# On-chip tiles of an attention and feed-forward kernel begin at multiples of 128 bytes

## The chip, the cores and the metric

The kernel runs on one core of one Trainium2 chip, as one program. The metric is the device time of one execution in microseconds (us). Before the change three runs took 1151.57, 1152.28 and 1153.96 us, a median of 1152.28 us.

## The reference

Attention over 4 batches, 12 heads, 448 positions and a head size of 64, with a root-mean-square norm of queries and keys, and then two feed-forward layers over the 1792 tokens of width 768, each with 2048 hidden columns:

```python
q_n, k_n = rmsnorm(q, g_q), rmsnorm(k, g_k)
attn = softmax(q_n @ k_n.T / sqrt(64))          # per batch and head
x = (attn @ v) as [1792, 768]
for w_in, w_out, beta in ((moe), 1.0), ((moe2), 1.702):
    h = x @ w_in
    x = (h * sigmoid(beta * h)) @ w_out
```

The weights come as 8-byte floats and are narrowed to 4 bytes on the chip; all else is 4-byte floats.

## The kernel before

**Stages.** Attention works through 24 pairs of heads (`NP`), and the feed-forward part through eight turns (u, p, g): layer u, half p of the tokens, half g of the hidden columns. While attention and the first turns run, the weights are loaded, narrowed (`block_narrow`), combined (`block_sum`) and stored to DRAM; each turn fetches them back in chunks of 128x768 through a ring of three (`fetch`, tiles f, wh, wl).

**Matmuls of the feed-forward part.** A 4-byte product is made of three matmuls of the type fp32r: every operand is split into a high part and a low part (wh, wl of the weights; th, tl of the first layer's input; bh, bl of the hidden values), and low x high, high x low and high x high are added up in PSUM. All of them are 128x128 weights (stationary) by 128x448 values (moving). Phase one of a turn (`one`, L857) forms seven sums of blocks in the order 1, 6, 2, 7, 5, 4, 3, with 28 tasks of nine matmuls, 252 in a turn; its moving tiles are th1 and tl1 for the first four tasks, th6 and tl6 for the next four, then th2, th7, th5, th4, th3 with their low parts. Phase two has 252 matmuls as well (`two`, L1009), in six turns, and 288 in the other two, the turns with u = 0 and g = 0 (`add_plain`, L952); there bh0 to bh3 and bl0 to bl3 are the moving tiles. That is 2016 + 1512 + 576 = 4104 fp32r matmuls. Of those of L857, 8 turns x 8 tasks x 9 = 576 have one of th1, tl1, th6 and tl6 as the moving tile.

**Attention's matmuls** (L626 scores, L730 values, the transposes at L691 to L705) are plain 4-byte matmuls, not fp32r.

**Order.** The kernel records tasks with estimated lengths, orders them in `emit`, and issues each engine's instructions in that order; the order is fixed when the program is built and nothing of it depends on addresses.

**Where tiles lie.** Pools grow from the left end of a partition (const, xp, wt, ring, rv, ap, then mw) or from its right end (sp, then tp and mg), and each tile begins at the next multiple of 32 bytes. The small tiles gcol, epsc (const), y (ap) and rr (ap), and ms and w (sp) have lengths that are no multiples of 128 bytes, and so set the begin of everything behind them. The usable length ends 32 bytes short of a multiple of 128. In the built program the begins are, as remainders of a division by 128 bytes:

| tiles | before | with the change |
|---|---|---|
| acc, t2, th1, tl1, th6, tl6 (left) | 64 | 0 |
| f, wh, wl, r of the weights; rows r0 to r11 of phase one and two | 64 | 0 |
| th2 to th5, th7 and their low parts (right) | 96 | 0 |
| bh0 to bh3, bl0 to bl3, g (right) | 96 | 0 |
| qk, sq, t, v, kn of attention (right) | 96 | 0 |
| e, ec, at, nb, rb of attention (left) | 32, 0 or 96 by tile | 0 |

Among attention's tiles at0 to at5 begin at 32 and at6 at 0, and rb0 (even pairs) at 0 and rb1 (odd pairs) at 96. In the feed-forward part th1 and th6 lie at 49,600 to 71,104 bytes of a partition and the weights at 74,176 to 98,752, while the b tiles begin at 137,952 or later and th2 and those behind it at 175,584 or later. Slices of a tile that matmuls read (448 moving columns, 128 columns of weights) are 1792 and 512 bytes, both multiples of 128.

Of the kernel before, what the change touches and what calls it, by code (L numbers as in the profile page):

```python
# [10 lines left out]
F32 = mybir.dt.float32  # L11
# [17 lines left out]
def kernel(  # L29
# [20 lines left out]
    NG = 2 * NK + 1  # L50
# [20 lines left out]
    def left(name):  # L71
        return ctx.enter_context(tc.tile_pool(name=name, bufs=1, reuse_waits="tile"))

    const = left("const")
# [5 lines left out]
    dp = ctx.enter_context(tc.tile_pool(name="dp", bufs=1, space=bass.MemoryType.DRAM))  # L80
    attn, early = ExitStack(), ExitStack()
    ap = attn.enter_context(tc.tile_pool(name="ap", bufs=1, reuse_waits="tile"))
    sp = early.enter_context(tc.tile_pool(name="sp", bufs=1, side="right", reuse_waits="tile"))

    ident = const.tile([128, 128], F32, name="ident")
    gcol = const.tile([128, 3], F32, name="gcol")
    epsc = const.tile([128, 1], F32, name="epsc")
    acc = xp.tile([128, NP2, KT, 2, 2 * HS], F32, name="acc")
    layers = ((moe_w_in, moe_w_out), (moe2_w_in, moe2_w_out))

    def engine(c):
        return {"p": nc.gpsimd, "v": nc.vector}[c]
# [4 lines left out]
    def bank(z):  # L97
        return ps.tile([128, 512], F32, tag=f"b{z}", name=f"b{z}")
# [3 lines left out]
    def task(eng, took, fn, reads=(), writes=(), lag=0.1, shared=False):  # L102
        x = len(todo)
        after = set()
        for r in reads:
            after |= {writer[r]} if r in writer else set()
        for r in writes:
            after |= {writer[r]} if r in writer else set()
            after |= readers.get(r, set())
        for r in reads:  # L110
            readers.setdefault(r, set()).add(x)
        for r in writes:
            writer[r], readers[r] = x, set()
        todo.append((eng, took, fn, sorted(after - {x}), lag, shared))
        return x
# [76 lines left out]
    held = {}  # L192
# [207 lines left out]
    def group(m):  # L400
        c, i = divmod(m, 2)
        return NK if c == NK else c + (NK + 1) * i

    def tile_of(key, pool, shape, dtype, tag):
        held[key] = pool.tile(shape, dtype, tag=tag, name=tag)
        return held[key]
# [30 lines left out]
    def norm(p, sides=(0, 1)):  # L437
        s = p % 2
        eng = "v" if p == 0 else "p"
        of = slice(sides[0], sides[-1] + 1)  # L440
        took = {"v": 0.27, "p": 0.56}[eng] * len(sides)

        def tiles():
            if 1 in sides:
                tile_of(("sq", p), sp, [128, 2, NG, D], F32, f"sq{s}")
                tile_of(("ms", p), sp, [128, 2, NG], F32, f"ms{s}")
                tile_of(("w", p), sp, [128, 2, NG], F32, f"w{s}")
                tile_of(("y", p), ap, [128, 2, NG], F32, f"y{p % 4}")

        def square(i):  # L450
            def fn():
                if i == sides[-1]:
                    tiles()
                t = held["qk", p].rearrange("p (i g d) -> p i g d", i=2, d=D)[:, i]
                engine(eng).tensor_tensor(held["sq", p][:, i], t, t, op=ALU.mult)
            return fn

        def fold():
            sq = held["sq", p][:, of]
            engine(eng).tensor_tensor(  # L460
                sq[:, :, :, :D // 2], sq[:, :, :, :D // 2], sq[:, :, :, D // 2:], op=ALU.add
            )

        def total():
            nc.vector.tensor_reduce(
                held["ms", p][:, of], held["sq", p][:, of, :, :D // 2], axis=AX.X, op=ALU.add
            )

        def root():
            w, y = (held[z, p][:, of] for z in "wy")  # L470
            nc.scalar.activation(
                out=w, in_=held["ms", p][:, of], func=ACTF.Ln, scale=1.0 / D, bias=epsc
            )
            nc.scalar.activation(out=y, in_=w, func=ACTF.Exp, scale=-0.5)

        def polish():
            ms, y, w = (held[z, p][:, of] for z in ("ms", "y", "w"))
            e = engine(eng)
            e.tensor_scalar(ms, ms, -0.5 / D, -0.5 * EPS, op0=ALU.mult, op1=ALU.add)
            e.tensor_tensor(w, y, y, op=ALU.mult)  # L480
            e.tensor_tensor(w, w, ms, op=ALU.mult)
            e.tensor_tensor(w, w, y, op=ALU.mult)
            e.tensor_scalar(y, y, 1.5, 0.0, op0=ALU.mult, op1=ALU.add)
            y, w = (held[z, p] for z in "yw")
            for i in reversed(sides):
                o = ry[(p + 1) % 2][:, 8:8 + NG] if i else y[:, 0]
                e.tensor_tensor(o, y[:, i], w[:, i], op=ALU.add)

        ms, y, sq = ([(*z, i) for i in sides] for z in (("ms", s), ("y", p % 4), ("sq", s)))
        for i in reversed(sides):  # L490
            task(eng, 0.535 if p == 0 else 1.11, square(i), reads=[("qk", s, i)], writes=[("sq", s, i)],
                 shared=True)
        task(eng, 2 * took, fold, writes=sq, shared=True)
        task("v", 0.27 * len(sides), total, reads=sq, writes=ms)
        task("a", 0.5, root, reads=ms, writes=y)
        task(eng, 0.75, polish, writes=ms + y + [("ryk", (p + 1) % 2)] * (1 in sides))
# [112 lines left out]
    def scores(p, c):  # L609
        nonlocal turns_s  # L610
        s = p % 2
        heads = range(1 if c == NK else 2)
        zs = [(turns_s + i) % 5 for i in heads]
        turns_s += len(zs)

        def mm():
            if c == 0:
                tile_of(("rr", p), ap, [128, 3, 8], F32, f"rr{p % 3}")
            pss = [bank(z)[:, :S] for z in zs]
            for i, t in enumerate(pss):  # L620
                held["s", p, 2 * c + i] = t
            t = held["t", p]
            cols = slice(128 * c, 128 * c + 128)
            for i, x in enumerate(pss):
                a = slice(0, 128) if c == NK else slice(64 * i, 64 * i + 64)
                nc.tensor.matmul(x, t[a, cols], t[a, NQ:], start=True, stop=True)  # L626

        task("pe", 0.76 if c == NK else 0.82, mm, reads=["ap"] + [("t", p % 4, y) for y in range(3)],
             writes=[("bank", z) for z in zs])
        for i, z in zip(heads, zs):  # L630
            m = 2 * c + i

            def top(m=m):
                nc.vector.tensor_reduce(  # L634
                    held["rr", p][:, 0, group(m):group(m) + 1], held["s", p, m], axis=AX.X,
                    op=ALU.max, negate=True,
                )

            def bias(m=m):
                g = slice(group(m), group(m) + 1)  # L640
                nc.gpsimd.tensor_tensor(  # L641
                    held["rr", p][:, 1, g], held["rr", p][:, 0, g], held["y", p][:, 0, g],
                    op=ALU.mult,
                )

            def exp(m=m, i=i):
                if c == NK:
                    o = tile_of(("ec", p), ap, [128, S], F32, f"ec{s}")
                else:
                    if i == 0:  # L650
                        tile_of(("e", p, c), ap, [128, 2, S], F32, f"e{s}{c}")
                    o = held["e", p, c][:, i]
                g = slice(group(m), group(m) + 1)
                nc.scalar.activation(  # L654
                    out=o, in_=held["s", p, m], func=ACTF.Exp, scale=held["y", p][:, 0, g],
                    bias=held["rr", p][:, 1, g], accum_out=held["rr", p][:, 2, g],
                )

            b, r = ("bank", z), ("rr", p % 3, m)
            task("v", 0.53, top, reads=[b, "ap"], writes=[r])  # L660
            task("p", 0.08, bias, reads=[("y", p % 4, 0)], writes=[r], lag=0.15)
            task("a", 0.72, exp, reads=[b, r, ("y", p % 4, 0), "ap"] + [("e", s, c, 0)] * i,
                 writes=[("e", s, c, z) for z in range(i, 2)] + [("sum", p % 3, m)])
# [502 lines left out]
```

## Time and profile before

| | |
|---|---|
| three runs | 1151.57, 1152.28, 1153.96 us (median 1152.28) |
| the profiled execution | 1150.59 us, of which its span is 1148.8 us |
| granted TensorE clock, mean | 0.992 of full speed |
| PE busy | 1110.5 us, 97% of the span |
| VectorE (DVE) busy | 929.3 us, 81% |
| ScalarE (ACT), GpSimd (POOL) busy | 724.5 us (63%), 380.8 us (33%) |
| feed-forward part | from 293.9 us of the span to its end |

The profile counts an instruction as busy from start to end, and matmuls of one engine overlap: a 128x448 matmul has a length of some 0.37 us, while the next begins some 0.2 us after it began. What a matmul costs where they follow each other without a gap is therefore read from starts, as the distance from one to the next, or from a piece of the chain of waits, whose length is divided by the matmuls in it. Rows of the chain give the start in the span, the length in us, and what ran. PEld is the load of the weights of the next matmul; L12 is line 12 of the kernel before.

### The profile page before, as it was taken

The page shows a single profiled execution, that of the slowest core. Times are in us where ns is not written, and L with a number is a line of the kernel's source. Part 1 is how long each engine was busy: PE and PEld are TensorE (multiplying, and loading weights), DVE is VectorE, ACT ScalarE, POOL GpSimd, SP SyncE. Part 2 cuts the span into 40 slices and gives each one's busy share as a digit, 9 for nine tenths or more (in the row PEclk, how much of TensorE's full clock was granted, in tenths as well). Part 3 has the DMA queues.
Part 4 walks back from the last instruction along what each step waited for, and adds up shares of the span by engine and source line. Part 5 has one row for each costly group of instructions (what it writes and reads, how often), then busy time and mean ns, then how long its engine had stood idle before and what let it go on. Part 6 is the DMA issues. An engine that isn't in the chain of part 4 may idle for free.

```text
span 1148.8 us, 17403 instructions
## 1 busy us (share of the span) xinstructions
PE 1110.5 (97%) x5601; PEld 914.6 (80%) x5601; DVE 929.3 (81%) x1448; ACT 724.5 (63%) x1371; POOL 380.8 (33%) x617
## 2 busy tenths in 40 slices
PE   4899899999999999999999999999999999999998
PEld 2454455555799999899999999999999999999997
DVE  5778888778796679997675999979989885885698
ACT  4677888888676676754766785366566544554452
POOL 5766666533221223314221100614212040420152
PEclk8899999999999999999999999999999999999999
DMA  7677887885747775567777656584583363333333
GB/s 238 187 258 222 272 266 227 253 263 189 236 137 245 240 235 155 162 205 238 250 244 239 211 178 200 155 266 145 185 254 104 122 195 105 102 107 113 99 108 124
DMA packets 178509, 222.09 MB, mean 193 GB/s; under 512 B 12329, under 2 KB 172274, under 8 KB 178418
## 3 DMA queue, kind: packets, MB, share of 16 engines
q1 hardware_dynamic: 178418, 220.98, 61.2%
q8 instruction: 44, 0.72, 0.3%
q14 instruction: 47, 0.39, 0.1%
HBM read 173.57 MB, written 47.36 MB: 192 GB/s over the span
## 4 chain that ended last, share of the span: by engine, by line
PE 77%; DVE 8%; DMA 6%; ACT 3%; issue 2%; POOL 2%; SPq 1%; DVEq 0%; ACTq 0%; POOLq 0%
PE b L857 35%; PE b L1009 22%; PE b L952 10%; PE b L626 3%; PE b L730 3%; DMA rb<-i 2%; PE b L705 2%; ACT e L654 1%; DVE bl L922 1%; DVE rr L634 1%; DVE wl L379 1%; DMA w<-r 1%; DMA i<-rt 1%; PE b L703 1%; DVE at L710 1%
## 5 line engine op out<-in xcount | busy, mean ns | idle before, releaser
L375 ACT CAST wh<-f 128x768 fp32r<-128x768 f32 x212 | 177.0, 835 | 155.2 <-PE b L857 96.6
L379 DVE TENSOR_TENSOR wl<-f,wh 128x768 fp32r<-128x768 f32 x212 | 227.7, 1074 | 55.1 <-ACT wh L375 51.6
L918 ACT CAST bh<-g 128x448 fp32r<-128x448 f32 x232 | 131.0, 566 | 111.0 <-PE b L1009 75.0
L922 DVE TENSOR_TENSOR bl<-g,bh 128x448 fp32r<-128x448 f32 x232 | 166.0, 727 | 41.2 <-ACT bh L918 39.3
L1009 PE MATMUL b<-bl,wh 128*128 128x448 f32 x504 | 186.2, 369 | 0.8 <-DVE bl L922 0.8
L1009 PE MATMUL b<-bh,wl 128*128 128x448 f32 x504 | 186.0, 369 | 0.3 <-DVE r L1035 0.2
L1009 PE MATMUL b<-bh,wh 128*128 128x448 f32 x504 | 185.6, 368 | 0.0
L238 POOL TENSOR_TENSOR r<-r 128x192 f32<-128x192 f32 x100 | 94.0, 945 | 258.7 <-DVE r L222 181.5
L857 PE MATMUL b<-th,wl 128*128 128x448 f32 x672 | 174.9, 369 | 0.0
L857 PE MATMUL b<-tl,wh 128*128 128x448 f32 x672 | 174.7, 369 | 0.0
L857 PE MATMUL b<-th,wh 128*128 128x448 f32 x672 | 174.6, 368 | 0.0
L857 PEld LDWEIGHTS b<-th,wl 128*128 128x128 f32 x672 | 126.5, 188 | 12.2 <-issue 0.7
L857 PEld LDWEIGHTS b<-th,wh 128*128 128x128 f32 x672 | 126.6, 188 | 11.6
L857 PEld LDWEIGHTS b<-tl,wh 128*128 128x128 f32 x672 | 126.6, 188 | 11.5
L905 POOL TENSOR_TENSOR g<-g,g 128x448 f32<-128x448 f32 x39 | 63.0, 1622 | 187.2 <-DVE g L905 100.9
L654 ACT ACTIVATE e<-b,rr,y 128x448 f32<-128x448 f32 x144 | 103.3, 721 | 18.8 <-POOL rr L641 18.5
L634 DVE TENSOR_REDUCE rr<-b 128x1 f32<-128x448 f32 x168 | 97.0, 615 | 19.7 <-PE b L626 19.4
L1009 PEld LDWEIGHTS b<-bl,wh 128*128 128x128 f32 x504 | 95.0, 188 | 11.0 <-DVE bl L922 2.3
L626 PE MATMUL b<-t 64*128 64x448 f32 (+1 forms) x336 | 99.1, 591 | 4.4 <-ACT e L654 3.6
L1009 PEld LDWEIGHTS b<-bh,wl 128*128 128x128 f32 x504 | 95.0, 188 | 9.9 <-DVE r L1035 1.0
L1009 PEld LDWEIGHTS b<-bh,wh 128*128 128x128 f32 x504 | 95.0, 188 | 8.7
L881 ACT ACTIVATE g<-g 128x448 f32<-128x448 f32 x96 | 54.8, 576 | 43.5 <-DVE g L877 43.3
(101 smaller groups left out, 1769.5 us busy)
## 6 DMA issues: line engine op xcount, KB each, us to landing
f<-w SPq DMA_DIRECT2D x212, 384.0 KB
r<-in_moe_w_in SPq DMA_DIRECT2D x64, 384.0 KB
w<-r SPq DMA_DIRECT2D x128, 192.0 KB
r<-in_moe_w_out SPq DMA_DIRECT2D x64, 384.0 KB
w<-r SPq DMA_DIRECT2D x56, 288.0 KB
t<-in_qkt SPq DMA_DIRECT2D x24, 480.0 KB
qk<-in_qk SPq DMA_DIRECT2D x48, 224.0 KB
v<-in_v SPq DMA_DIRECT2D x24, 256.0 KB
```

Source lines behind the costliest of these rows:

```text
L238: engine(e).tensor_tensor(x[:, o], x[:, a], x[:, b], op=op)
L375: nc.scalar.copy(held[w][0], held[f])
L379: nc.vector.tensor_tensor(l, held[f], f32(h), op=ALU.subtract)
L626: nc.tensor.matmul(x, t[a, cols], t[a, NQ:], start=True, stop=True)
L634: nc.vector.tensor_reduce(held["rr", p][:, 0, group(m):group(m) + 1], held["s", p, m], axis=AX.X, op=ALU.max, negate=True,)
L654: nc.scalar.activation(out=o, in_=held["s", p, m], func=ACTF.Exp, scale=held["y", p][:, 0, g], bias=held["rr", p][:, 1, g], accum_out=held ...
L857: nc.tensor.matmul(held[pb], x[:, c0:c0 + 128], y[:, k], start=bool(start and c == 0), stop=(c == 3 * KH - 1), skip_group_check=True,)
L905: engine(e).tensor_tensor(held[o], held[x], held[y], op=op)
L918: nc.scalar.copy(held[r][0], held[src])
L922: nc.vector.tensor_tensor(l, held[src], h.bitcast(F32), op=ALU.subtract)
L952: nc.tensor.matmul(held["plain", z], x[:, ms], y, start=(q == 0 and t == 0 and c == 0), stop=(q == GROUP - 1 and t == 1 and c == 2), skip_ ...
L1009: nc.tensor.matmul(held["p", 5 if i == 3 else i, m], x[:, c0:c0 + 128], y, start=(i != 3 and q2 == 0 and c == 0), stop=(q2 == GROUP - 1 an ...
```

## The change

Five edits, and nothing else: a pad of 24 words at the right end of the partition (`side`), so that the right-hand tiles begin 96 bytes lower; gcol and epsc leave the pool const and share a padded tile of 32 words in ap (`small`), so that acc and what follows begin 64 bytes lower; the tiles ms, w and y become 4x8 words, of which 2x7 are used as before; and rr becomes 4x8 words in place of 3x8.

```diff
     ap = attn.enter_context(tc.tile_pool(name="ap", bufs=1, reuse_waits="tile"))
+
+    ident = const.tile([128, 128], F32, name="ident")
+    side = ctx.enter_context(tc.tile_pool(name="side", bufs=1, side="right", reuse_waits="tile"))
+    side.tile([128, 24], F32, name="side")
     sp = early.enter_context(tc.tile_pool(name="sp", bufs=1, side="right", reuse_waits="tile"))
-
-    ident = const.tile([128, 128], F32, name="ident")
-    gcol = const.tile([128, 3], F32, name="gcol")
-    epsc = const.tile([128, 1], F32, name="epsc")
+    small = ap.tile([128, 32], F32, name="small")
+    gcol, epsc = small[:, 0:3], small[:, 3:4]
     acc = xp.tile([128, NP2, KT, 2, 2 * HS], F32, name="acc")
...
                 tile_of(("sq", p), sp, [128, 2, NG, D], F32, f"sq{s}")
-                tile_of(("ms", p), sp, [128, 2, NG], F32, f"ms{s}")
-                tile_of(("w", p), sp, [128, 2, NG], F32, f"w{s}")
-                tile_of(("y", p), ap, [128, 2, NG], F32, f"y{p % 4}")
+                for z, pool, tag in (("ms", sp, s), ("w", sp, s), ("y", ap, p % 4)):
+                    t = tile_of((z, p), pool, [128, 4, 8], F32, f"{z}{tag}")
+                    held[z, p] = t[:, :2, :NG]
...
-                tile_of(("rr", p), ap, [128, 3, 8], F32, f"rr{p % 3}")
+                tile_of(("rr", p), ap, [128, 4, 8], F32, f"rr{p % 3}")
```

No engine gets another order, another count of instructions or another wait: row by row the programs differ only in the names gcol and epsc (now small) and in the shape of the few norm instructions that read or write ms, w and y, which is 128x2x7 in place of 128x14 (L465, L471, L474 and L479 to L483, once for each of 23 pairs).

## Rows read from the trace of the kernel before

**Rows 1.** The page: span and busy time of each engine.

```profile
span 1148.8 us, 17403 instructions
...
PE 1110.5 (97%) x5601; PEld 914.6 (80%) x5601; DVE 929.3 (81%) x1448; ACT 724.5 (63%) x1371; POOL 380.8 (33%) x617
```

**Rows 2.** The page: the chain that ended last, by engine and by line.

```profile
PE 77%; DVE 8%; DMA 6%; ACT 3%; issue 2%; POOL 2%; SPq 1%; DVEq 0%; ACTq 0%; POOLq 0%
PE b L857 35%; PE b L1009 22%; PE b L952 10%; PE b L626 3%; PE b L730 3%; DMA rb<-i 2%; PE b L705 2%; ACT e L654 1%; DVE bl L922 1%; DVE rr L634 1%; DVE wl L379 1%; DMA w<-r 1%; DMA i<-rt 1%; PE b L703 1%; DVE at L710 1%
```

**Rows 3.** The chain in order of time: start us, length us, engine, line, count.

```profile
349.42 59.52 PE b L952 x288
408.94 51.79 PE b L857 x252
460.73 8.80 PE b L1009 x43
...
484.45 27.88 PE b L1009 x138
...
623.65 36.93 PE b L857 x180
...
699.12 19.69 PE b L1009 x95
...
779.78 52.08 PE b L1009 x252
```

**Rows 4.** Timeline of PE, th6 then (from 423.37) th2: start us, length us.

```profile
421.54 0.77 PE L857 MATMUL b<-th,wl 128*128 128x448 f32 x3
422.15 0.77 PE L857 MATMUL b<-tl,wh 128*128 128x448 f32 x3
422.76 0.77 PE L857 MATMUL b<-th,wh 128*128 128x448 f32 x3
423.37 0.78 PE L857 MATMUL b<-th,wl 128*128 128x448 f32 x3
423.99 0.78 PE L857 MATMUL b<-tl,wh 128*128 128x448 f32 x3
```

**Rows 5.** Timeline of PE, th1 in the first turn.

```profile
295.22 0.78 PE L857 MATMUL b<-th,wh 128*128 128x448 f32 x3
295.84 0.78 PE L857 MATMUL b<-th,wl 128*128 128x448 f32 x3
```

**Rows 6.** Timeline of PE, L1009 around a wait in the second turn.

```profile
482.48 0.37 PE L1009 MATMUL b<-bh,wh 128*128 128x448 f32 x1
482.69 0.37 PE L1009 MATMUL b<-bl,wh 128*128 128x448 f32 x1
...
485.17 0.36 PE L1009 MATMUL b<-bh,wl 128*128 128x448 f32 x1
485.37 0.36 PE L1009 MATMUL b<-bh,wh 128*128 128x448 f32 x1
```

**Rows 7.** Timeline of PEld, the loads of weights in that stretch.

```profile
485.17 0.19 PEld L1009 LDWEIGHTS b<-bh,wh 128*128 128x128 f32 x1
```

**Rows 8.** Windows of turns two and four: us, PE, PEld, DVE, ACT, POOL busy.

```profile
409.00:512.20 103.20, 103.04 (x505) 94.68 (x504) 95.81 (x141) 69.94 (x117) 31.28 (x26) 1.00 0.60 191
...
623.50:727.90 104.40, 104.25 (x506) 94.83 (x505) 96.44 (x161) 70.83 (x117) 8.88 (x7) 1.00 0.62 196
```

**Rows 9.** Costliest groups, by shape: the low parts of the weights.

```profile
L379 DVE TENSOR_TENSOR wl<-f,wh 128x768 fp32r<-128x768 f32 x212 | 227.7, 1074 | 55.1 <-ACT wh L375 51.6 <-DMA f<-w 0.3
```

**Rows 10.** One line each, L730 and L738: duration ns min/median/max.

```profile
L730 PE MATMUL b<-at,v x384: 538/540/591, 41.7 to 304.2; 128*64 128x448 f32 x192
...
L738 DVE TENSOR_TENSOR acc<-b,rb x24: 611/624/626, 45.2 to 304.8; 128x448 f32<-128x448 f32 x24
```

**Rows 11.** Groups by shape: small POOL instructions of the norm.

```profile
L481 POOL TENSOR_TENSOR w<-w,ms 128x14 f32<-128x14 f32 x23 | 5.6, 244 | 1.8
...
L487 POOL TENSOR_TENSOR y<-y,w 128x7 f32<-128x7 f32 x23 | 5.0, 219 | 0.0
```

## The prediction, made before the changed kernel ran

> **What bounds the kernel now.** I read the page first: PE is busy for 1110.5 of 1148.8 us, VectorE (DVE) for 929.3 [rows 1]. The chain that ended last runs over PE for 77% of the span, and the three lines of the feed-forward part alone (L857, L1009, L952) hold 35, 22 and 10% of it; DVE has 8%, DMA 6% [rows 2]. A change that only moves tiles leaves every instruction where it is, so it can act through one thing, the time that an instruction takes by the place of its operands. The question is therefore which instructions have shown such a dependence, and here the trace of before holds a test of its own, since its tiles do not all begin at the same remainder by 128 bytes.
>
> The next view is the chain in order of time, where gapless pieces give the distance between matmuls: 288 of L952 take 59.52 us, 252 of L1009 take 52.08 us, both 206.7 ns each; but 252 of L857 take 51.79 us, 205.5 ns [rows 3]. The timeline shows where L857 gains: while th6 is the moving tile, three matmuls take 0.61 us (421.54 to 422.15 to 422.76 to 423.37, 203 ns each), and from the first matmul of th2 at 423.37 on 0.62 us (206.7 ns) [rows 4]. The weights come from the same ring on both sides of the switch, and no wait lies there. With 180 of the 252 at 206.7 ns, the 72 of th1 and th6 are left with 51.79 - 37.20 = 14.59 us, 202.6 ns. So a moving tile at remainder 64 costs 202.6 ns, one at 96 costs 206.7 ns.
>
> Two stretches do not fit a rule by address alone. In the first turn th1 itself goes at 0.62 us for three [rows 5]. And after a wait in the second turn L1009, with its tiles at 96 as before, goes at 200 ns (485.17 to 485.37), where 0.21 us stood ahead of the wait (482.48 to 482.69) [rows 6]. So the pace also depends on how the loads of weights and the matmuls fall together: a load begins with a matmul and takes 0.19 us [rows 7], and the next matmul follows its end by a few ns more or less. The pace has levels, and begin and history together pick one.
>
> **The change, part by part.**
>
> *Matmuls of the feed-forward part.* All 4104 get moving tiles and weights at remainder 0, which no fp32r row of before shows. Nearest is remainder 64 (202.6 ns); the ends are 200.0 ns, the best pace in the trace, and 206.7 ns, the common one. I take 202.6 ns, since th1 and th6 hold it in seven of eight turns, because 0 shares with 64 that it is a multiple of 64, and since weights and moving tile have the same remainder there, as they will everywhere. Matmuls with a tile at 96: 1440 of L857 (2016 - 576), 576 of L952, 1512 of L1009, in all 3528. Of the L1009 I leave out 280: the 138 that follow 484.45 [rows 3] and about as many after other waits, which go at 200 to 205 ns already. Saved: 3248 x 4.1 ns = 13.3 us. The 138 lose 2.6 ns each, 0.4 us. Sum: -12.9 us.
>
> *What DVE gives back.* In turns two and four DVE is busy for 95.81 of 103.20 and 96.44 of 104.40 us [rows 8], and there the chain leaves PE: from 469.5 (460.73 + 8.80) to 484.45, and from 660.6 (623.65 + 36.93) to 699.12 [rows 3], 15 + 38.5 = 53.5 us in which a faster PE only waits longer. That loses 2% of 53.5, 1.0 us. If DVE sets the time from the start of those turns on, it is 75.5 us in each (408.94 to 484.45, 623.65 to 699.12), 3.0 us. Late next would be the low parts that DVE makes, bl (L922) and wl (L379), the latter 212 x 1074 ns and waiting on DMA for 0.3 us only [rows 9]. I take the middle, 2.0 us; a turn at 202.6 ns needs 102.1 us, still above DVE's 96.
>
> *Attention.* Its matmuls are not fp32r. All of L730's 384 lie between 538 and 591 ns with a median of 540 [rows 10], though at6 begins at 0 and at0 to at5 at 32: a quarter of them already stands where the change puts all, and it gains at most 2 ns. L738 reads rb at 0 in even pairs and at 96 in odd ones and has 611, 624 and 626 ns as least, middle and most [rows 10]. So engines outside the feed-forward matmuls: 0, bounds -0.4 and +0.4 us (24 x 15 ns). The norm's shape 2x7 in place of 14: between 7 and 14 elements an instruction takes 219 and 244 ns [rows 11], so 0 to 25 ns, over 5 POOL instructions in each of 23 pairs at most 2.9 us of POOL, which is busy a third of the span [rows 1] and makes norms three pairs ahead; if that cover were gone, it would be those 2.9 us. I take 0.
>
> *DMA.* No row separates transfers by begin. Its 6% of the chain are 69 us [rows 2], all of it in attention. Were they to move by the same 2% as the matmuls, it would be 1.4 us either way; I take 0.
>
> *A rule against the change.* Begins at 64 and at 96 differ by 4.1 ns [rows 4]. The Trainium skill, page "SBUF — State Buffer", section "Specifications (TRN2)", states lines of 16 bytes, with a cost for each crossing to a new one. All begins before are multiples of 32, hence of 16, so by this rule no operand touches fewer lines afterwards and the sum would be 0 instead of -12.9 us. The trace disagrees as far as th6 and th2 go, which both begin on such a line. It is kept as a rival below, as a matter of where tiles lie.
>
> **Sum.** Against the profiled execution's own time, 1150.6 us: -12.9 + 2.0 = 1139.7 us. The median of the three runs is 1.7 us above that execution, so the forecast for a median is 1141 us (1139 to 1144 with DVE's bounds and a pace 0.4 ns off).
>
> **The rivals.**
>
> *Remainder 0 gives the best pace, 200.0 ns.* For: this pace holds for over a hundred matmuls in a row [rows 3, 6], so nothing of the array forbids it. Against: no address in the trace brings it about, only a wait. 3248 x 6.7 + 576 x 2.6 + some 0.3 = 23.6 us, less DVE's share at 3.2% (1.7 to 4.9, say 3.3): 1152.3 - 20.3 = 1132 us; without any give-back 1129 us.
>
> *Not the remainder but the region.* th1 and th6 lie at the left, next to the weights; th2 and all b tiles lie far to the right. If that is what sets 202.6 against 206.7, the change keeps both groups where they are and nothing happens: 1152 us. For: in the trace of before remainder and region go together. (By the lines of 16 bytes that the Trainium skill states, above, it would be the same 1152 us.) Against: L1009 at 200 ns with tiles at the right [rows 6] shows that the region does not forbid a better pace.
>
> *History decides, and the slow level wins: slower.* Today each turn passes from tiles at 96 to tiles at 64 and back, and at each entry into th1 the pace is set anew. With one remainder for all there is no such switch, and whatever pace the first matmuls of the feed-forward part fall into lasts. In the first turn that is 206.7 ns, with th1 and the weights at the same remainder [rows 5]. Then the 576 lose 4.1 ns (2.4 us) and the 138 and their like 6.7 ns or less (1.2 us): 1152.3 + 3.6 = 1156 us. It decides if three matmuls take 0.62 us at the end of the first turn and waits do not break it.
>
> **How the numbers follow.** Something over 0.2% (2.3 us) can be told from no change here. Chances: forecast 0.41, best pace 0.28 (mixtures of both count with the nearer), region 0.14, history 0.13; 0.04 for a cost that I do not see, slower. Faster is 0.41 + 0.28 = 0.69, less than 2.3 us either way 0.14, slower 0.13 + 0.04 = 0.17. The range goes from 1129 us, the best pace without give-back, to 1153 us, which takes in the region case; it leaves out the slower ones, 0.17. The likeliest case's own range is 1139 to 1144 us.
>
> **What would show it.** In the profile of the changed kernel: pieces of 252 matmuls of L857 at 51.1 us and of L1009 at 51.1 us (50.4 for the best pace; 51.8 and 52.1 if the region rules; 52.1 for both if history does), no step of pace between th6 and th2, matmuls of attention at the same 540 ns, and DVE's share of turns two and four up by a point or two with waits of PE there that are no shorter. I am wrong if th2 still goes at 0.62 us for three, or if the pace is better and the time is not, which would put the loss on DVE in more turns than two.

## The result, and the profile after

The change took 1139.91 us (median of six runs, 1136.97 to 1141.83) against 1151.59 us before (six runs beside them, 1148.1 to 1153.96): a ratio of 0.990, 95% interval 0.9879 to 0.9922. The profiled execution took 1141.83 us, its span is 1140.0 us; before it was 1150.59 and 1148.8 us. The forecast was 1141 us, in a range from 1129 to 1153.

The page of the changed kernel answers to [rows 1] and [rows 2]:

```profile
span 1140.0 us, 17403 instructions
...
PE 1101.3 (97%) x5601; PEld 910.4 (80%) x5601; DVE 929.3 (82%) x1448; ACT 724.3 (64%) x1371; POOL 381.9 (34%) x617
...
PE 76%; DVE 9%; DMA 7%; issue 3%; ACT 2%; SPq 2%; POOL 1%; DVEq 0%; ACTq 0%; POOLq 0%
```

Counts are the same, DVE's 929.3 us too, ACT's and POOL's times within 1.1 us; PE is busy for 9.2 us less, its loads of weights (PEld) for 4.2 us less, and the span is shorter by 8.8 us. The chain in order of time answers to [rows 3] (start us, length us, engine, line, count; every line is two higher than before, so L857 is now L859, L952 L954 and L1009 L1011; in the kernels of the experiments zero to four higher):

```profile
348.11 58.37 PE b L954 x288
406.48 48.83 PE b L859 x241
...
481.27 28.78 PE b L1011 x138
510.05 52.08 PE b L859 x252
562.12 59.52 PE b L954 x288
621.64 37.21 PE b L859 x180
...
697.39 28.26 PE b L1011 x138
725.65 51.07 PE b L859 x252
776.73 51.07 PE b L1011 x252
827.80 51.07 PE b L859 x252
```

Divide each length by its count. (A piece that begins at a wait also holds some 0.26 us of that wait, so the 28.78 us of 138 matmuls are 28.52 at 206.7 ns each and the rest.) 58.37 us for 288 are 202.7 ns, and 51.07 us for 252 are 202.7 ns, whether the line is L859 or L1011: the forecast's pace and its two pieces of 51.1 us. But from 481.27 to the wait ahead of 697.39 the same lines go at 206.7 ns (52.08 for 252, 59.52 for 288, 37.21 for 180), with the same tiles at the same places. The stretch begins at one wait of PE and ends at the next; added up from the starts it has 1042 matmuls. Before, most of it had 206.7 ns as well, and th1, th6 and the 138 behind the wait less [rows 3], so here the change loses: 697.39 - 481.27 = 216.12 us from wait to wait, where it was 699.12 - 484.45 = 214.67. The granted clock is 1.00 in this stretch and in the quick one behind it (windows 481.27:697.30 and 725.70:1083.00), so it does not make the difference. By the prediction's own sign of being wrong, th2 at 0.62 us for three, it was wrong in turns three and four.

The timeline of PE around the switch from th6 to th2 (72 matmuls after 406.48, so at 421.07) answers to [rows 4]:

```profile
420.30 0.77 PE L859 MATMUL b<-th,wh 128*128 128x448 f32 x3
420.90 0.77 PE L859 MATMUL b<-th,wl 128*128 128x448 f32 x3
421.51 0.77 PE L859 MATMUL b<-tl,wh 128*128 128x448 f32 x3
422.12 0.77 PE L859 MATMUL b<-th,wh 128*128 128x448 f32 x3
422.73 0.56 PE L859 MATMUL b<-th,wl 128*128 128x448 f32 x2
```

Three matmuls take 0.60 or 0.61 us on both sides; the step to 0.62 us is gone.

### The profile page after: what moved, and what is told of

Read it like the earlier page. It is cut to its first block, busy times and chain, and to the rows that moved or that the text cites. A ratio compares the mean times of both kernels' runs of the same rounds, so it can differ in the third digit from the quotient of the medians.

```text
span 1140.0 us, 17403 instructions
## 1 busy us (share of the span) xinstructions
PE 1101.3 (97%) x5601; PEld 910.4 (80%) x5601; DVE 929.3 (82%) x1448; ACT 724.3 (64%) x1371; POOL 381.9 (34%) x617
## 4 chain that ended last, share of the span: by engine, by line
PE 76%; DVE 9%; DMA 7%; issue 3%; ACT 2%; SPq 2%; POOL 1%; DVEq 0%; ACTq 0%; POOLq 0%
PE b L859 35%; PE b L1011 21%; PE b L954 10%; PE b L628 4%; DMA rb<-i 3%; PE b L732 3%; PE b L707 2%; DVE bl L924 1%; DVE rr L636 1%; DVE wl L381 1%; DMA i<-rt 1%; DMA w<-r 1%; PE b L705 1%; SPq L534 1%; DVE g L907 1%
## 5 line engine op out<-in xcount | busy, mean ns | idle before, releaser
L1011 PE MATMUL b<-bl,wh 128*128 128x448 f32 x504 | 184.7, 366 | 1.1 <-DVE bl L924 1.0
L1011 PE MATMUL b<-bh,wl 128*128 128x448 f32 x504 | 184.7, 366 | 0.8 <-DVE r L1037 0.6
L1011 PE MATMUL b<-bh,wh 128*128 128x448 f32 x504 | 184.4, 366 | 0.0
L240 POOL TENSOR_TENSOR r<-r 128x192 f32<-128x192 f32 x100 | 93.3, 939 | 259.3 <-DVE r L224 187.7
L859 PE MATMUL b<-th,wl 128*128 128x448 f32 x672 | 173.4, 366 | 0.0
L859 PE MATMUL b<-tl,wh 128*128 128x448 f32 x672 | 173.2, 366 | 0.0
L859 PE MATMUL b<-th,wh 128*128 128x448 f32 x672 | 173.2, 366 | 0.0
L859 PEld LDWEIGHTS b<-th,wl 128*128 128x128 f32 x672 | 126.1, 188 | 11.3 <-issue 0.7
L859 PEld LDWEIGHTS b<-th,wh 128*128 128x128 f32 x672 | 126.2, 188 | 10.6
L859 PEld LDWEIGHTS b<-tl,wh 128*128 128x128 f32 x672 | 126.2, 188 | 10.6
L1011 PEld LDWEIGHTS b<-bl,wh 128*128 128x128 f32 x504 | 94.7, 188 | 9.9 <-DVE bl L924 2.1
L1011 PEld LDWEIGHTS b<-bh,wl 128*128 128x128 f32 x504 | 94.7, 188 | 9.5 <-DVE r L1037 1.5
L1011 PEld LDWEIGHTS b<-bh,wh 128*128 128x128 f32 x504 | 94.7, 188 | 7.7
```

The lines of the kernel that those rows point to most:

```text
L240: engine(e).tensor_tensor(x[:, o], x[:, a], x[:, b], op=op)
L859: nc.tensor.matmul(held[pb], x[:, c0:c0 + 128], y[:, k], start=bool(start and c == 0), stop=(c == 3 * KH - 1), skip_group_check=True,)
L1011: nc.tensor.matmul(held["p", 5 if i == 3 else i, m], x[:, c0:c0 + 128], y, start=(i != 3 and q2 == 0 and c == 0), stop=(q2 == GROUP - 1 an ...
```

## The experiments

Four theories stood against each other. **Own begin** (the forecast's): a moving tile at a multiple of 64 bytes gets the better pace. **Region**: the place in the partition, not the remainder. **Relation**: what counts is how far the moving tile begins from the weights, as a remainder (at first by 128 bytes). **History**: after a wait the pace falls into one of several levels and stays there until the next wait or the next change of tile.

The attention part ended at a different time in each profiled execution: the first fp32r matmul starts at 292.6, 292.9 and 293.4 us in three executions of the changed kernel, and between 292.5 and 298.4 us in the others, with no order by begin. So beside the times the table at the end of this section gives the feed-forward part alone (span less that start).

**The change once more**, no edit.

> The changed kernel once more, nothing altered. If the begin of the tiles alone set the pace, the pieces of the chain would repeat: turns three and the first part of turn four at 206.7 ns per fp32r matmul (59.5 us for 288 of L954), the rest at 202.7 ns. If history decides (what the pace falls into after a wait lasts until the next wait), those turns may as well go at 202.7 ns (58.4 us for 288), and the time with them: 1137 us without the slow stretch, 1142 us with it.

1137.51 us, and the chain has no slow stretch between the waits:

```profile
480.46 28.24 PE b L1011 x138
508.70 51.07 PE b L859 x252
559.77 58.37 PE b L954 x288
```

The same program with the same addresses went at 202.7 ns where the execution above went at 206.7. So one and the same program has both levels, and the execution decides between them.

**Only the left tiles moved** (weights, th1, th6 at 0; right tiles stay at 96). In this and later kernels the identity matrix moves to another pool to make room.

```diff
-    ident = const.tile([128, 128], F32, name="ident")
-    side = ctx.enter_context(tc.tile_pool(name="side", bufs=1, side="right", reuse_waits="tile"))
-    side.tile([128, 24], F32, name="side")
...
     small = ap.tile([128, 32], F32, name="small")
+    ident = ap.tile([128, 128], F32, name="ident")
```

> Left half of the change alone: weights, th1 and th6 at remainder 0, all right-hand tiles (th2 and on, b) at 96 as before; the identity lies in the attention pool to make room. Own begin of the moving tile: th2 and on and b at 206.7 ns, th1 and th6 at 202.7, time as before, 1150 to 1154 us. Weights' begin: all at 202.7 ns, 1138 to 1142 us. Relation of weights and moving tile: right-hand tiles at 206.7 ns, as before.

1147.59 us (ten runs, 1146.35 to 1151.57), ratio 0.9973 (0.9958 to 0.9988). The chain has

```profile
728.18 51.56 PE b L857 x252
779.74 51.74 PE b L1009 x252
```

so the right-hand tiles, which did not move at all, went from 206.7 to 205.3 ns (51.74 / 252). Their own begin and their region are those of before; of these matmuls' operands only the weights, th1 and th6 have a new begin. None of the three theories had forecast 205.3 ns.

**Only the right tiles moved** (right at 0; weights, th1, th6 stay at 64).

```diff
-    ident = const.tile([128, 128], F32, name="ident")
+    const.tile([128, 16], F32, name="lpad")
     side = ctx.enter_context(tc.tile_pool(name="side", bufs=1, side="right", reuse_waits="tile"))
...
+    ident = ap.tile([128, 128], F32, name="ident")
```

> Right half alone: right-hand tiles at 0, weights, th1 and th6 at 64 as before. Own begin of the moving tile, multiples of 64: all at 202.7 ns, time 1137 to 1142 us as with the whole change. Relation of weights and moving tile by 128 bytes: right-hand tiles at 206.7 ns, about 1152 us. Only remainder 0 for both: the same, 1152 us.

1137.54 us (five runs, 1135.49 to 1143.76), ratio 0.9902 (0.9866 to 0.9938). In its chain

```profile
727.13 51.27 PE b L860 x252
778.40 50.96 PE b L1012 x252
```

L1012 has 202.2 ns, and if L860's 180 with right-hand tiles have it too, the 72 of th1 and th6 are left with 51.27 - 36.40 = 14.87 us, 206.5 ns. th1, th6 and the weights all lie 512 bytes lower than before, so their remainders and the distance between them are unchanged, and yet th1 and th6 lost what they had before (202.6 ns, [rows 3]): now the right-hand tiles are quick and the left ones slow. The time is the one that own begin had forecast, and the relation by 128 had missed it (206.7 ns for the right-hand tiles, 1152 us); but the begin of the tile alone can't make th1 and th6 slow.

**All begins at 32.**

```diff
+    const.tile([128, 8], F32, name="lpad")
...
-    side.tile([128, 24], F32, name="side")
+    side.tile([128, 16], F32, name="side")
```

> All tiles at remainder 32. Own begin of the moving tile: no tile is at a multiple of 64 now, all at 206.7 ns but for stretches behind waits, 1152 to 1156 us. Relation of weights and moving tile: both have the same remainder, all at 202.7 ns, 1137 to 1142 us.

Two pieces of its chain:

```profile
721.14 51.08 PE b L860 x252
772.21 51.07 PE b L1012 x252
```

The pace of the change, 202.7 ns, without one tile at a multiple of 64. The median is 1141.86 us over ten runs, but they reach from 1137.03 to 1153.49 (ratio 0.9941, 0.9908 to 0.9973). What the change needs is one remainder for weights and moving tiles, not the remainder 0; by which unit of bytes, the last two kernels show.

**Weights moved against the moving tiles.** In five kernels the moving tiles keep the remainders of the change (th1 and th6 lie 512 bytes lower), and a pad of 8, 16, 24, 32 or 56 words shifts the weights' ring and the pools behind it:

```diff
     for i in ORDER[:2]:
         t_tile(wt, i)
+    wt.tile([128, 16], F32, name="wpad")
```

*By 64 bytes, and the change beside it on the same chip.*

> All moving tiles (th1, tl1, th6, tl6 too) begin at 0, the weights wh and wl 64 bytes after a multiple of 128, so that no switch between tiles changes how the two begins stand to each other. Relation theory (the pace is set by the moving tile's begin against the weights', and a distance of 64 keeps the lower pace, as th2 to th7 showed in the run before): 202.7 ns throughout, pieces of 252 of L859 and of L1011 at 51.1 us, about 1137 us, and less spread than the change itself, since 206.7 never appears. History theory (a wait decides, whatever the begins): stretches at 206.7 between two waits as in the profile of the change, 1137 to 1153 us with the same spread as all at 32. Own-begin theory: as the change, 1140 us.

> The change itself on the same chip, for comparison with the three others: 1137 to 1143 us in most runs; history theory: its runs fall into groups about 4 us apart (a stretch of some 1,000 matmuls between two waits at 206.7 or at 202.7 ns).

The chain of the kernel with weights 64 bytes further:

```profile
722.13 50.96 PE b L860 x252
773.09 50.96 PE b L1012 x252
```

That is 202.2 ns, 0.5 below the relation theory's forecast, and no stretch of its chain has another pace: 1134.85 us (five runs, 1133.96 to 1138.65), ratio 0.9883 (0.9865 to 0.9902), faster than both kernels. The change beside it had 1143.44 us (eleven runs, 1139.09 to 1151.21), ratio 0.9956 (0.9931 to 0.998), and in its profiled execution the other stretch was slow, from the wait in the fourth turn to the one near the end, as its chain shows:

```profile
618.43 36.49 PE b L859 x180
693.26 28.78 PE b L1011 x138
722.04 52.08 PE b L859 x252
774.12 52.08 PE b L1011 x252
```

The forecast 4 us between groups of runs can't be read from eleven times. Note the change's two intervals: 0.9879 to 0.9922 in the result above and 0.9931 to 0.998 here do not touch, though it is one program. What they leave out is how often an execution falls into a slow stretch.

*The same distance at other begins:* moving tiles at 96 with weights at 32 (the edit below, which also takes out the pad `side`), and moving tiles at 64 with weights at 0 (pads of 16 words for `lpad` and 8 for `side`).

```diff
+    const.tile([128, 24], F32, name="lpad")
...
+    wt.tile([128, 16], F32, name="wpad")
```

> All moving tiles at 96, the weights at 32: distance 64. Own-begin theory (a tile at 96 costs 206.7 or 205.3 ns): pieces of 252 at 51.8 to 52.1 us, 1148 to 1152 us. Relation theory: pieces of 252 at 51.1 us, about 1137 us.

> All moving tiles at 64, the weights at 0: a distance of 64 as in the kernel with weights at 64, from the other side. Relation theory: 202.2 ns throughout as there, pieces of 252 at 50.9 to 51.1 us, no stretch at 206.7, 1134 to 1138 us. Were only one side of the distance good: 204.5 to 206.7 ns, 1146 to 1152 us.

1138.30 and 1138.51 us (two runs each; ratios 0.9905, 0.9882 to 0.9928, and 0.9907, 0.9877 to 0.9936). Both chains have pieces of 252 at 50.96 us as above. A moving tile at 96, the slow place of before, has 202.2 ns when the weights begin at 32.

*By 32 bytes.*

> All moving tiles at 0, the weights at 32: distance 96, an odd multiple of 32. Own-begin theory: 202.7 ns as every tile at 0, pieces of 252 at 51.1 us, about 1138 us. Relation theory: the higher pace, 204.5 to 206.7 ns, pieces of 252 at 51.5 to 52.1 us, 1146 to 1152 us.

1145.39 us (eight runs, 1140.53 to 1153.27), ratio 0.9975 (0.9951 to 1.0); the moving tiles as in the change, and yet 204.4 ns in its chain:

```profile
727.91 51.52 PE b L860 x252
779.43 51.52 PE b L1012 x252
```

*By 96 bytes.*

> All moving tiles at 0 as in the change, the weights 96 bytes after a multiple of 128, so that a moving tile begins 32 after the weights in terms of 128, as th2 to th7 and b* did in the kernel before. Relation theory: the pace of before everywhere, 206.7 ns with stretches at 200 or 204.5 after waits, pieces of 252 near 52.1 us, 1146 to 1153 us, although every moving tile begins at a multiple of 128. Own-begin theory: 202.7 ns, about 1138 us.

Neither theory had this: 200.0 ns, the best pace, in all turns, and 1129.06 us in the profiled execution. The other of its two runs, 1137.2 us, has no profile; ratio 0.986 (0.982 to 0.9899). Its chain:

```profile
717.65 50.40 PE b L860 x252
768.05 50.40 PE b L1012 x252
```

The relation theory had been stated in terms of 128, by which this kernel's distance is that of th2 and b* before. The tiles and their slices are multiples of 256 too, though, so the distance can be taken by 256: before, th2 less the weights is 175,584 - 74,176 = 101,408, which leaves 32; here it leaves 160. The last two kernels separate the two units.

*By 128 bytes* (distance 0 by 128, as in the change; 128 by 256).

> The kernel of weights at 64 with a pad of 128 bytes in place of 64: distance 0 in terms of 128 again, all else alike. Relation theory with history: as the change, each stretch between two waits at 202.7 or at 206.7 ns, runs spread from 1136 to 1153 us, median 1138 to 1144, above that of weights at 64 (1134.85). If the other pool of the identity or the wider gap itself had made the gain of weights at 64: 1134 to 1138 us in every run.

1145.83 us (twelve runs, 1141.63 to 1147.34), ratio 0.9962 (0.9947 to 0.9977). Neither 202.7 nor 206.7 ns but 204.0 in every turn, so 128 is not the unit; and since only the pad's length differs, neither the pad nor the identity's other pool made the gain of the kernel with 64 bytes. Its chain:

```profile
727.65 51.41 PE b L860 x252
779.06 51.41 PE b L1012 x252
```

*By 224 bytes* (32 by 128, as with 96 bytes; 32 by 256 too, as th2 and b* had before the change).

> The kernel with weights at 96 and 128 bytes more of pad: the moving tiles begin 32 after the weights in terms of 256, as th2 to th7 and b* did in the kernel before; in terms of 128 nothing differs from weights at 96. Relation theory by 256 (so far 0: 202.7 or 206.7; 96: 205.3; 128: 203.6; 160: 200; 192: 202.2; 224: 204.5): the pace of before in its main stretches, pieces of 252 at 51.8 to 52.1 us with shorter stretches at 200 or 204.5 after waits, 1146 to 1153 us. Relation theory by 128: 200 ns as with weights at 96, pieces of 252 at 50.4 us, 1129 to 1137 us. History theory by itself, where the switch from th1 and th6 held before at 206.7: 200 ns here too, since no tile stands otherwise than the others.

1147.49 us (twelve runs, 1139.31 to 1152.4), ratio 0.9963 (0.9939 to 0.9987); the profiled execution took 1152.4. Its chain:

```profile
305.76 43.41 PE b L860 x216
...
408.12 52.08 PE b L860 x252
...
728.79 52.08 PE b L860 x252
780.87 52.08 PE b L1012 x252
```

206.7 ns in nearly all of it, as before the change, though every moving tile begins at a multiple of 128; and the first stretch, up to a wait in L955, has 43.41 / 216 = 201.0 ns, nearly the 200 that before had behind one wait [rows 6]. By 128 this kernel would have been the quickest of all; by 256 it is the kernel before. The pair alone would leave a rival: distance 32 by 128 could have both levels, 200 and 206.7, and each profiled execution its own draw. Against it, both runs with 96 bytes (1129.06 and 1137.2 us) lie below all twelve with 224 (lowest 1139.31); the kernel with 128 bytes has 204.0 ns in every long stretch, which no long stretch of the change has; and 205.3 ns (left only) stands against 204.4 (weights by 32), both 96 by 128 but 96 and 224 by 256. So of the two units it is 256.

All profiled executions, with the distance of the moving tiles from the weights by 256 bytes (th1 and th6 / the others, where they differ), and the pace from their chains; each median stands beside runs of before with medians from 1148.85 to 1151.59:

| kernel | distance | ns in turns five to eight | feed-forward part, us | median, us (runs) |
|---|---|---|---|---|
| before | 0 / 32 | 202.6 / 206.7 | 854.9 | 1151.59 (6) |
| the change | 0 | 202.7, 206.7 in turns three and four | 846.6 | 1139.91 (6) |
| the change once more | 0 | 202.7 | 843.1 | 1137.51 (1) |
| the change beside the others | 0 | 206.7, 202.7 up to turn four | 851.0 | 1143.44 (11) |
| all at 32 | 0 | 202.7 | 843.1 | 1141.86 (10) |
| left only | 0 / 96 | 202.6 / 205.3 | 851.3 | 1147.59 (10) |
| right only | 0 / 192 | 206.5 / 202.2 | 843.6 | 1137.54 (5) |
| weights by 128 | 128 | 204.0 | 848.2 | 1145.83 (12) |
| weights by 96 | 160 | 200.0 | 834.5 | 1133.13 (2) |
| weights by 64 | 192 | 202.2 | 841.8 | 1134.85 (5) |
| weights 32, moving 96 | 192 | 202.2 | 841.5 | 1138.30 (2) |
| weights 0, moving 64 | 192 | 202.2 | 841.7 | 1138.51 (2) |
| weights by 32 | 224 | 204.4 | 849.8 | 1145.39 (8) |
| weights by 224 | 32 | 206.7 | 855.6 | 1147.49 (12) |

## Why the prediction was right, and where it was not

**The matmuls, -12.9 us.** The mechanism held: no instruction was added or taken away, and the time came from the distance between the starts of matmuls. Added up over the fp32r matmuls (pauses left out), these distances are 841.1 us before (4087 of them), 832.9 in the profiled execution (4089) and 829.0 in the change once more (4090): 205.79, 203.69 and 202.69 ns on average, which over 4104 matmuls is -8.6 and -12.7 us against -12.9. The whole feed-forward part gained 8.3 and 11.8 us. In stretches without a slow level the size was right: turns five to the middle of eight took 1091.40 - 727.99 = 363.41 us before (to the start of the last L1009, by the same chain), and 1083.16 - 725.65 = 357.51 after; 1764 - 288 matmuls at 4.1 ns would be 6.05, and 5.90 were saved.

**The reason given for it was partly wrong.** The step that failed is "a moving tile at remainder 64 costs 202.6 ns, one at 96 costs 206.7 ns". It read two places beside each other as a rule on the place. The runs show a rule on the distance from the weights: a tile at 96 has 202.2 ns with the weights at 32, and a tile at 0 has 206.7 with the weights shifted by 224 bytes. Of the three reasons for taking 202.6 ns, that 0 is a multiple of 64 falls (all at 32 does the same). That weights and moving tile have the same remainder stands only by 256, and the prediction counted by 128: with weights by 128 all begins have remainder 0 by 128 as in the change, and the pace is 204.0 ns. That the change brings the distance to 0 by 256 too (101,408 - 96 + 64 = 101,376, which is 396 x 256) was not worked out beforehand. So 1141 us came out partly by luck: in that, and in how many stretches fell into the quick level, which nothing before the change could tell.

**History** was put down as a rival for the whole kernel (0.13: all matmuls in the slow level). It acts by stretches between waits, and in part of the executions: 4 us of the forecast were missing in this profiled execution through 1042 matmuls x 4 ns. It bears on why the change's own time is not one number: 1139.91 us over six runs and 1143.44 over eleven, both in the likeliest case's own range, 1139 to 1144. That the slower runs of those eleven (up to 1151.21) had slow levels in more stretches is argued from the profiled ones; they have no profile.

**DVE's give-back, +2.0 us** (1.0 to 3.0). The right place, but too large a term. PE's waits in the second phase, 0.8 for bl and 0.2 us for r before, are in the waits view of the changed kernel (line waited for, us in total, times, longest)

```profile
PE b L1011 <- DVE bl L924: 1.0, 1, 1.0
...
PE b L1011 <- DVE r L1037: 0.6, 1, 0.6
```

and 1.1 and 1.3 us in the change once more: +0.6 and +1.4 us, the first of them below the lower bound. With weights by 96, at 200 ns, they are

```profile
PE b L1012 <- DVE r L1038: 3.0, 2, 1.8
...
PE b L1012 <- DVE bl L925: 1.5, 1, 1.5
```

4.5 us, +3.5, where 3.3 were taken for that pace. DVE's share of turns two and four, in the windows from the start of each turn to that of the next, answers to [rows 8]:

```profile
406.50:510.00 103.50, 102.89 (x505) 94.52 (x505) 96.60 (x143) 69.48 (x117) 31.64 (x26) 1.00 0.62 193
621.60:725.60 104.00, 103.89 (x506) 94.48 (x505) 96.38 (x161) 70.85 (x117) 8.75 (x7) 1.00 0.62 196
```

93.3% and 92.7%, from 92.8 and 92.4: half a point at most, where one or two were expected. The first of these turns ended and the second ran in the slow stretch; in the change once more, without it, the shares are 92.6% and 94.4% (95.44 of 103.02 and 97.33 of 103.10 us), so that only turn four shows the rise.

**Attention and DMA, 0.** The rows of these two lines in the changed kernel, durations least, middle and most, answer to [rows 10]:

```profile
L732 PE MATMUL b<-at,v x384: 538/539/591, 40.7 to 303.6; 128*64 128x448 f32 x192
...
L740 DVE TENSOR_TENSOR acc<-b,rb x24: 609/624/625, 44.2 to 304.2; 128x448 f32<-128x448 f32 x24
```

The groups of the norm by shape answer to [rows 11] (L489 is not one of those whose shape changed):

```profile
L483 POOL TENSOR_TENSOR w<-w,ms 128x14 f32<-128x14 f32 x23 | 5.6, 242 | 1.8
...
L489 POOL TENSOR_TENSOR y<-y,w 128x7 f32<-128x7 f32 x23 | 5.0, 218 | 0.0
```

These rows are the same as before within 2 ns. The other four POOL instructions with the new shape (L481, L482, L484, L485) went from 209, 236, 262 and 219 to 230, 232, 245 and 253 ns; with L483 that is 32 ns over all five, 0.7 us of POOL for 23 pairs, where at most 2.9 had been allowed. In the change once more L485 has 226 ns and L484 261, so single groups differ as much between executions of one program, and no cost of the 2x7 shape can be told from that. The feed-forward part began 0.5 us earlier (293.4 for 293.9 us), less than the 0.8 us by which three executions of the change differ.

**Region** is refuted: the right-hand tiles, not moved, changed their pace when the weights moved, and with the same tiles in the same region the feed-forward part took from 834.5 to 855.6 us by the length of one pad. By the lines of 16 bytes of the Trainium skill (page "SBUF — State Buffer", section "Specifications (TRN2)") alone all these kernels would be equal, since all begins are multiples of 32; the runs disagree by these 21.1 us.

**Best pace** came true, but not for the change: at distance 160 the feed-forward part is 20.4 us shorter than before, and 20.3 had been worked out.

**What stays open.** Distance 64 was not tried, and no unit above 256: the slices of a moving tile lie 1792 bytes apart, which is a multiple of 256 and not of 512, so every kernel has both remainders by 512 (before, the right-hand tiles at 32 and at 288 by 512 both had 206.6 ns). Distances 96, 128, 160 and 224 stand in one kernel and one profiled execution each; the other runs have no profile, and at 224 the eight runs reach from 1140.53 to 1153.27 us, so a second level there is not excluded. Distance 160 has two runs only, one of them 8 us slower. What in the chip makes the distance matter, and what picks the level at a wait, is not shown.

## What to carry to other kernels

Where fp32r matmuls follow each other without a gap, read the distance between their starts for each pair of moving tile and weights, and treat the begin of the one relative to the other as a parameter to try: here one pad of 16 words ahead of the weights, on top of the change and of the identity's move, gave 1134.85 us against 1143.44 for the change on the same chip, with intervals that do not touch (0.9865 to 0.9902, and 0.9931 to 0.998); the change's first six runs (0.9879 to 0.9922) do touch the first of them. A round number of bytes for everything is only one such setting, and here one whose level could change at a wait. When two groups of tiles differ in pace, write down all that differs between them, the partner operand too, before a rule is made of one of them; and profile the same kernel more than once.

## What the runs showed of the hardware

128x448 fp32r matmuls with a new load of weights each had paces from 200.0 to 206.7 ns, by the distance by 256 bytes between moving tile and weights: 160 gave 200.0, 192 gave 202.2, 224 gave 204.4, in steps of 2.2 ns for 32 bytes; 96 gave 205.3 and 128 gave 204.0. At 0 there are two levels, 202.7 and 206.7, and at 32 mainly two as well, near 200 and 206.7; in these traces a pace that had held for long changed at a wait or at a change of distance. At 200.0 and at 206.7 ns nearly every single distance from start to start is that within 2 ns; the paces between are means of unequal distances, with weights by 128 for example 209, 196, 203, 212 and 200 ns over and over (mean 204.0), so that a pace is read over many matmuls and not from one. The load itself lasted 187 to 189 ns in all of them.
